# Reordering the head of a fused retention and gated MLP kernel: w_in's u half cast by GpSimd alone, the split of b behind the second k cast, centring as a step of its own

## The chip, the cores and the metric

The kernel runs on one core of one Trainium2 chip. The metric is the device time of one execution in microseconds (us), as the median of several runs. The core's engines are TensorE (PE in the profile; its weight loads are PEld), VectorE (DVE), ScalarE (ACT) and GpSimd (POOL); SyncE (SP) issues most transfers. Each engine works through its own queue in order and waits on semaphores for the others.

## The reference, cut to what matters

Retention (attention with a decay per head in place of a softmax) over q, k, v of shape 8 x 8 x 576 x 64, then a gated MLP whose gate mixes positions:

```
ret = (q k^T / 8) * gamma_h^(t-s)  for t >= s, else 0
x   = (ret v), heads side by side                 # 8 x 576 x 512
h   = gelu_tanh(x @ w_in)                         # w_in 512 x 1024
u, v = h[..., :512], h[..., 512:]
v_n = (v - mean(v)) / sqrt(var(v) + 1e-6) * g_ln
v_s = w_sg @ v_n (over positions, 576 x 576) + b_sg
out = x + (u * v_s) @ w_out                       # w_out 512 x 512
```

Inputs and output are float32; the matrix products inside are bf16.

## The kernel before, in words

**Tiling.** The positions of a batch are a lead of 64 and two blocks of 256. The leads of four batches are put together as one block, so the eight batches give 18 blocks j: block 0 is the leads of batches 0 to 3, blocks 1 and 2 are batch 0, 3 and 4 are batch 1, and so on. A block has two chunks c of 128 positions each.

**Stages of a block.** `load` issues the transfers of k, q and v. `cast(j, part, engine)` scales q and k by powers of gamma and turns them into bf16 (L263, a product with a table), v by a plain copy (L245). `T` transposes q or k on TensorE (`tp`) and copies it to SBUF (ScalarE for k, VectorE for q). `Sc(j, g)` makes scores for half of the heads and VectorE multiplies them by the causal mask (L300, `ret`). `Z(j, c)` adds to the running state and copies it to `zb`. `inter` and `intra` form the outputs from the state and from the masked scores; the end of `intra` copies them to `xT`, chunk 0 by ScalarE and, in the first three blocks, chunk 1 by VectorE.

**Stages of a chunk.** `V(j, c)` multiplies by the v half of w_in (L365) and applies the activation (L368, `vg`). `stats` takes mean and variance on VectorE (L376 to L380, `rs`) and then centres and scales by g (L385, `vc`); `power` raises the variance to -1/2 on GpSimd (L372, called pow below); `norm` multiplies the two on ScalarE (L393, L397, `vnm` and `vn`). `U(j, c)` is the u half (L414, L417). `W(b, c, half)` multiplies the normalized v of a batch by the transposed w_sg (`wT`, and `wL` for the lead, which also carries b; L434) and VectorE multiplies by u (L436, `gT`). `O` is the output product (L443) and the residual (L446), copied by ScalarE and stored.

**Weights.** w_in is loaded in two halves as float32 (`wst`), v half first, and cast to bf16 in four pieces. `split_b` clears the unused halves of `wL` and splits b into three bf16 parts `bp` (L169 to L176). `place_b(e)` issues three small transfers from `bp` into `wL[e]` on the GpSimd queue (L191). `load_w(j)` issues the transfers of w_sg there (L198), and `build_wT` transposes it on TensorE (L205), copied out by VectorE or ScalarE through a pool of two PSUM buffers that `T` and `Sc` use as well.

**Order.** The schedule is manual: engines take instructions in the order of the calls. Blocks 0 to 2, the head, are written out call by call (from L480 on). From block 3 on a loop interleaves the stages, with W and O products drawn from a list. `spin(n)` is n matmuls on zeros whose result isn't used. Steps registered with `later(n, f)` run after n calls of `tick`, which T, V, U, W and O make at their ends; in the head `stats_of`, `pow_of` and `norm_of` hold the steps of chunk 2j + c instead, and are called by hand. Chunk 1 (of block 0) is left to ticks 14, 16 and 18 after the head.

**Names in the argument.** "Cast 2k" is `cast(2, "k", ...)`; "pow2", "vc2" and "rs2" are the steps of chunk 2 (block 1, c = 0), and likewise chunks 3, 4 and 5. The first W in TensorE's order multiplies with wT[0] to wT[3] and then wL[0]; its "fourth matmul" needs the last transposed weight and the `vn` of chunk 5.

Of the kernel before, what the change touches and what calls it, by code (L numbers as in the profile page):

```python
# [13 lines left out]
I32 = mybir.dt.int32  # L14
# [5 lines left out]
def kernel(  # L20
# [12 lines left out]
    nc = tc.nc  # L33
# [6 lines left out]
    GB, LEAD, NT, MID = 4, 64, 9, 4  # L40
# [7 lines left out]
    consts = ctx.enter_context(tc.tile_pool(name="consts", bufs=1))  # L48
# [46 lines left out]
    srow_i = consts.tile([128, 3, 2], I32, name="srow_i")  # L95
    nc.gpsimd.iota(srow_i[:, 0], pattern=[[1, 2]], base=0, channel_multiplier=2)
    nc.gpsimd.iota(srow_i[:, 1:], pattern=[[256, 2], [1, 2]], base=LEAD, channel_multiplier=2)

    srow_i = consts.tile([128, 3, 2], I32, name="srow_i")
    nc.gpsimd.iota(srow_i[:, 0], pattern=[[1, 2]], base=0, channel_multiplier=2)  # L100
    nc.gpsimd.iota(srow_i[:, 1:], pattern=[[256, 2], [1, 2]], base=LEAD, channel_multiplier=2)
# [34 lines left out]
    w_stage = {}  # L136
# [31 lines left out]
    def split_b():  # L168
        nc.gpsimd.memset(wL[0][64:], 0.0)  # L169
        nc.gpsimd.memset(wL[1][:64], 0.0)  # L170
        rest = bs
        for n in range(3):
            nc.gpsimd.tensor_copy(bp[:, n, :], rest[:])
# [10 lines left out]
    def fill_first():  # L184
        nc.gpsimd.memset(vnm[0][0][64:], 1.0)
        nc.gpsimd.memset(vnm[0][1][:64], 1.0)

    def place_b(e):
        for n in range(3):
            r = 64 * (1 - e) + n  # L190
            nc.gpsimd.dma_start(wL[e][r:r + 1, :], bp[:SB * 2 - 1, n, :] if e else bp[1:, n, :])  # L191
# [39 lines left out]
    def later(n, fn):  # L231
        pend.append([n, fn])
        pend.sort(key=lambda e: e[0])
# [13 lines left out]
    def cast(j, part, eng):  # L247
        s = blk.setdefault(j, {})
        qk, vf = loaded[j]
        b, half = place(j)[1:]  # L250
        kind = 0 if b is None else 1 + half
        if part == "q":
            dst, src, tab = w2.tile([128, 2, H, D], BF, name="qb"), qk[:, 0], gq
        else:
            pool = consts if b is None else w3
            dst = pool.tile([128, 2, H, D], BF, name=part + ("lead" if b is None else "b"))
            src, tab = (qk[:, 1], gk) if part == "k" else (vf[:], None)
        s[part + "b"] = dst
        o = dst[:].rearrange("p a h d -> p h a d")
        if tab is None:  # L260
            copy(eng, o, src)
        else:
            eng.tensor_tensor(o, src, tab[:, kind].rearrange("p a h -> p h a").unsqueeze(3).to_broadcast(  # L263
                [128, H, 2, D]), op=Alu.mult)
# [94 lines left out]
    stats_of, pow_of, norm_of = {}, {}, {}  # L359

    def V(j, c, wait=(2, 4)):
        p, m = chunk(j, c)
        hv = psD.tile([128, F2], F32, name="hv", tag="d")
        for kk in range(KK):
            nc.tensor.matmul(hv[:], xTs[p][:, kk, 128 * m:128 * m + 128], w_in[:, kk, F2:],  # L365
                             start=(kk == 0), stop=(kk == KK - 1))
        vg = vgp.tile([128, F2], F32, name="vg")
        nc.scalar.activation(vg[:], hv[:], Act.Gelu_apprx_tanh)  # L368
        st = {}

        def power():
            nc.gpsimd.tensor_tensor(st["rs"][:], st["rs"][:], mhalf[:], op=Alu.pow)  # L372

        def stats():
            bst = w3.tile([128, 6], F32, name="bst")
            nc.vector.bn_stats(bst[:], vg[:])  # L376
# [3 lines left out]
            nc.vector.tensor_scalar(rs[:], mv[:, 1:2], 1e-6, None, op0=Alu.add)  # L380
            st["rs"] = rs
            if wait:
                power()
            vc = w2.tile([128, F2], F32, name="vc")
            nc.vector.scalar_tensor_tensor(vc[:], vg[:], mv[:, 0:1], g_bc[:], op0=Alu.subtract, op1=Alu.mult)  # L385
            st.update(vc=vc)

        def norm():
            rs, vc = st["rs"], st["vc"]
            if m == MID:  # L390
                for e in range(2):
                    half = slice(64 * e, 64 * e + 64)
                    nc.scalar.mul(vnm[p % 3][e][half], vc[half], rs[half])  # L393
                vns[p, m] = vnm[p % 3]
            else:
                vn = vnp.tile([128, F2], BF, name="vn")
                nc.scalar.mul(vn[:], vc[:], rs[:])  # L397
                vns[p, m] = [vn, vn]

        if wait:  # L400
            later(wait[0], stats)
            later(wait[1], norm)
        else:
            stats_of[2 * j + c], pow_of[2 * j + c], norm_of[2 * j + c] = stats, power, norm
        tick()

    def U(j, c):
# [79 lines left out]
    T(0, "q")  # L487
    spin(3)
    cast(0, "v", nc.gpsimd)
    split_b()  # L490
    Sc(0, 0)
    Sc(0, 1)
    Z(0, 1)
# [4 lines left out]
    inter(0)  # L498
    intra(0)
    load(3)  # L500
    nc.gpsimd.memset(wnat[:, :, 0:64], 0.0)
    place_b(0)
    cast(1, "q", nc.vector)
    build_g()
    V(0, 0, None)
# [1 line left out]
    T(1, "k")  # L507
    T(1, "q")
    cast(1, "v", nc.gpsimd)
    spin(2)  # L510
    Sc(1, 0)
    Z(1, 0)
    cast(2, "k", nc.gpsimd)
# [9 lines left out]
    for j in range(SB):  # L523
        load_w(j)
    cast(2, "v", nc.gpsimd)
    for n in range(2):
        (nc.gpsimd.tensor_copy if n else nc.scalar.copy)(w_in[:, :, 256 * n:256 * n + 256], w_stage[0][:, :, 256 * n:256 * n + 256])
    V(1, 0, None)
    Sc(2, 0)
    V(1, 1, None)  # L530
    Z(2, 0)
    inter(2)
    fill_first()
    stats_of[0]()
    pow_of[0]()
    Sc(2, 1)
    Z(2, 1)
    cast(3, "k", nc.gpsimd)
    wb = ["L0", "L1"] + list(range(SB - 1))
    U(0, 0)  # L540
    norm_of[0]()
    stats_of[2]()
    pow_of[2]()
    U(0, 1)
    intra(2)
    U(1, 0)
    norm_of[2]()
    stats_of[3]()
    cast(3, "q", nc.gpsimd)
    pow_of[3]()  # L550
    V(2, 0, None)
    V(2, 1, None)
    load(5)
    build_wT(wb[0])
    norm_of[3]()
    U(1, 1)
    build_wT(wb[1])
    stats_of[4]()
    cast(3, "v", nc.gpsimd)
    place_b(1)  # L560
    pow_of[4]()
    build_wT(wb[2])
    U(2, 0)
    build_wT(wb[3])
    stats_of[5]()
    pow_of[5]()
    norm_of[4]()
    build_wT(wb[4])
    U(2, 1)
    build_wT(wb[5])  # L570
# [23 lines left out]
    cast(5, "v", nc.gpsimd)  # L594
    fill_consts()
    later(14, stats_of[1])
    later(16, pow_of[1])
    later(18, norm_of[1])

# [74 lines left out]
```

## Time and profile before

| | us |
|---|---|
| median of 3 runs | 234.67 |
| the three runs | 234.67, 234.17, 237.1 |
| profiled execution | 234.34 |
| its span, first to last instruction | 232.6 |
| TensorE busy in the span | 215.0 |
| VectorE / ScalarE / GpSimd busy | 165.8 / 134.7 / 129.4 |
| granted TensorE clock, mean | 0.995 of full |

A row of a timeline reads: start, duration (both us from the span's start), engine, line, operation, output and inputs by the program's names, shape, count, and in brackets how long the engine stood idle before it and what ended that wait. Rows with a count hold several instructions one after the other. A group of busy times by stage gives, for each stretch, its length and the busy time and instruction count of each engine, then the granted clock, the share of the DMA engines and GB/s.

### The profile page before, as it was taken

The numbers are of one execution on the slowest core, as the hardware profiler recorded it, in microseconds if no ns is written. First come the engines' busy times: TensorE is split into PE (matmuls) and PEld (weight loads), VectorE is DVE, ScalarE is ACT, GpSimd is POOL, SyncE is SP. The second block draws the span as 40 slices with busy tenths as digits, with TensorE's granted clock in tenths as the row PEclk, the third lists the DMA queues.
The fourth block names the chain that finished last, engine by engine and source line by source line (L and its number), as shares of the span: only waits on it lengthen the run. The fifth ranks groups of instructions, "written<-read, shape, count | busy, mean of one in ns | idle before, by whom it ended". The sixth has DMA issues, their size and how long they took to land.

```text
span 232.6 us, 8357 instructions
## 1 busy us (share of the span) xinstructions
PE 215.0 (92%) x3603; PEld 154.8 (67%) x3603; DVE 165.8 (71%) x357; ACT 134.7 (58%) x217; POOL 129.4 (56%) x130
## 2 busy tenths in 40 slices
PE   7796879789997999999999899999999999999991
PEld 3344476577776786777768677777777777667760
DVE  5476788688979896579767886779857985566320
ACT  5353568614669464946575757657394739466332
POOL 5298869799958485538555674939381611113000
PEclk9999999999999999999999999999999999999997
DMA  6999999999396993699249922869522003300344
GB/s 167 286 301 297 302 258 275 238 282 268 94 261 204 201 230 65 207 278 291 79 126 299 276 74 66 251 213 287 146 90 93 4 3 111 118 3 0 136 116 159
DMA packets 64261, 41.59 MB, mean 179 GB/s; under 512 B 2208, under 2 KB 58592, under 8 KB 64224
## 3 DMA queue, kind: packets, MB, share of 16 engines
q1 hardware_dynamic: 61664, 39.33, 62.6%
q0 software_dynamic: 1472, 1.20, 3.1%
q10 hardware_dynamic: 1088, 0.52, 1.0%
q8 instruction: 28, 0.46, 0.9%
q14 instruction: 9, 0.07, 0.1%
HBM read 32.79 MB, written 9.44 MB: 182 GB/s over the span
## 4 chain that ended last, share of the span: by engine, by line
PE 67%; ACT 7%; DVE 6%; DMA 6%; POOL 5%; SPq 5%; issue 1%; ACTq 1%; DVEq 0%; POOLq 0%
PE wp L434 15%; PE op L443 13%; PE hv L365 10%; PE hu L414 10%; PE tp L272 5%; SPq L91 5%; DMA wst<-in_moe_w_in_dram 4%; PE op L446 3%; POOL rs L372 3%; PE zp L321 3%; PE sc L296 3%; PE ot L348 3%; PE ot L337 3%; DMA qk<-in_q_dram 2%; DVE bst L376 2%; ACT vnm L393 2%
## 5 line engine op out<-in xcount | busy, mean ns | idle before, releaser
L372 POOL TENSOR_TENSOR rs<-rs,mhalf 128x1 f32<-128x1 f32 x36 | 33.0, 916 | 73.0 <-DVE rs L380 67.9
L300 DVE TENSOR_TENSOR ret<-sc,mask 128x512 bf16<-128x512 f32 x72 | 46.2, 684 | 12.9 <-PE sc L296 12.8
L434 PE MATMUL wp<-wT,vn 128*128 128x288 bf16 x256 | 41.7, 287 | 2.9 <-ACT vn L397 2.8
L436 DVE TENSOR_TENSOR gT<-wp,uT 128x288 bf16<-128x288 f32 x64 | 28.1, 453 | 16.8 <-PE wp L434 14.0
L365 PE MATMUL hv<-w_in,xT 128*128 128x512 bf16 x144 | 36.5, 379 | 2.4 <-ACT xT L245 2.4
L414 PE MATMUL hu<-xT,w_in 128*128 128x128 bf16 x576 | 37.8, 219 | 0.0
L443 PE MATMUL op<-w_out,gT 128*128 128x512 bf16 x144 | 37.1, 380 | 0.0
L414 PEld LDWEIGHTS <-w_in 128*128 128x128 bf16 x576 | 34.0, 98 | 1.9
L368 ACT ACTIVATE vg<-hv 128x512 f32<-128x512 f32 x36 | 21.4, 596 | 22.5 <-PE hv L365 22.3
L376 DVE BATCH_NORM_STATS2 bst<-vg 128x6 f32<-128x512 f32 x36 | 24.8, 689 | 12.1 <-ACT vg L368 11.9
L449 ACT COPY ob<-op 128x512 f32<-128x512 f32 x36 | 20.9, 586 | 20.5 <-PE op L446 18.0
L263 POOL TENSOR_TENSOR kb<-qk,gk 128x1024 bf16<-128x1024 f32 x16 | 31.1, 1941 | 2.8 <-DMA qk<-in_k_dram 2.8
L397 ACT ACTIVATE vn<-vc,rs 128x512 bf16<-128x512 f32 x32 | 23.1, 722 | 14.4 <-POOL rs L372 12.4
L434 PEld LDWEIGHTS <-vn 128*128 128x128 bf16 x256 | 23.8, 98 | 10.7 <-ACT vn L397 3.7
L385 DVE SCALAR_TENSOR_TENSOR vc<-vg,mv,g_bc 128x512 f32<-128x512 f32 x36 | 29.9, 830 | 0.2 <-issue 0.2
L263 POOL TENSOR_TENSOR qb<-qk,gq 128x1024 bf16<-128x1024 f32 x15 | 28.9, 1929 | 0.0
L417 ACT ACTIVATE uT<-hu 128x512 bf16<-128x512 f32 x36 | 21.7, 602 | 11.5 <-PE hu L414 11.5
L245 ACT CAST xT<-ot 128x512 bf16<-128x512 f32 x33 | 22.0, 733 | 1.8 <-PE ot L348 1.6
L245 ACT COPY kT<-tp 128x1024 bf16<-128x1024 bf16 x18 | 18.1, 1008 | 8.3 <-PE tp L272 8.3
L365 PEld LDWEIGHTS <-xT 128*128 128x128 bf16 x144 | 12.8, 98 | 13.7 <-ACT xT L245 4.0
L443 PEld LDWEIGHTS <-gT 128*128 128x128 bf16 x144 | 12.3, 98 | 9.5
L434 PE MATMUL wp<-wL,vnm 128*128 128x288 bf16 x64 | 18.4, 287 | 0.0
(95 smaller groups left out, 290.0 us busy)
## 6 DMA issues: line engine op xcount, KB each, us to landing
qk<-in_k_dram SPq DMA_DIRECT2D x16, 512.0 KB, 8.2
qk<-in_q_dram SPq DMA_DIRECT2D x16, 512.0 KB, 7.5
vf<-in_v_dram SPq DMA_DIRECT2D x16, 512.0 KB, 7.6
out_dram<-ob SPq DMA_DIRECT2D x32, 256.0 KB, 2.5
wst<-in_moe_w_in_dram SPq DMA_DIRECT2D x2, 1024.0 KB, 7.3
vf<-in_v_dram SPq DMA_DIRECT2D x8, 128.0 KB, 4.3
out_dram<-ob SPq DMA_DIRECT2D x8, 128.0 KB, 2.4
qk<-in_k_dram SPq DMA_DIRECT2D x6, 128.0 KB, 3.4
```

The costliest lines, as they stand in the source:

```text
L245: (eng.copy if eng is nc.scalar else eng.tensor_copy)(o, i)
L263: eng.tensor_tensor(o, src, tab[:, kind].rearrange("p a h -> p h a").unsqueeze(3).to_broadcast([128, H, 2, D]), op=Alu.mult)
L300: nc.vector.tensor_tensor(s["ret"][:, r, 2 * g:2 * g + 2], sc[r][:], msk[:].unsqueeze(1).to_broadcast([128, 2, 2, 128]), op=Alu.mult)
L365: nc.tensor.matmul(hv[:], xTs[p][:, kk, 128 * m:128 * m + 128], w_in[:, kk, F2:], start=(kk == 0), stop=(kk == KK - 1))
L372: nc.gpsimd.tensor_tensor(st["rs"][:], st["rs"][:], mhalf[:], op=Alu.pow)
L376: nc.vector.bn_stats(bst[:], vg[:])
L385: nc.vector.scalar_tensor_tensor(vc[:], vg[:], mv[:, 0:1], g_bc[:], op0=Alu.subtract, op1=Alu.mult)
L397: nc.scalar.mul(vn[:], vc[:], rs[:])
L414: nc.tensor.matmul(hu[:, c, :], w_in[:, kk, 128 * c:128 * c + 128], xTs[p][:, kk, 128 * m:128 * m + 128], start=(kk == 0), stop=(kk == KK ...
L434: nc.tensor.matmul(ps[:], vns[p, m][e][:, 128 * c:128 * c + 128], w, start=(x == 0), stop=(x == SB - 1))
L436: nc.vector.tensor_tensor(gTs[p][:, c, col:col + HS], ps[:], uTs[p][:, c, col:col + HS], op=Alu.mult)
L443: nc.tensor.matmul(op[:], gTs[p][:, c, r], w_out[:, c, :], start=(c == 0), stop=False, skip_group_check=True)
```

## The change

- A repeated pair of iotas that fill `srow_i` is removed.
- `split_b` no longer clears `wL`; that and the clearing of w_sg's padding (`wnat`) are a function `clear_wL`, called where `split_b` was, behind cast 0v. `split_b` is called behind cast 1k on GpSimd, after `load(3)`.
- `place_b(0)` moves from there to behind cast 1v; the spin(2) at that place is removed.
- Both pieces of w_in's u half are cast by GpSimd; ScalarE did the first. `fill_first` (two clearings of `vnm`) moves ahead of them.
- Centring is taken out of `stats` as a step `centre`. For chunk 2 it is called behind `intra(2)`, for the others in the head right behind the statistics, with pow behind it; for chunk 1 it has a tick of its own.
- Casts 3k, 3q and 3v move behind the pow steps of chunks 2, 3 and 4; the statistics of chunks 4 and 5 move ahead of the second and the fourth `build_wT`. `place_b(1)` now follows pow5.

```
--- before.py
+++ after.py
@@ -91,10 +91,6 @@
                 nc.sync.dma_start(dst[:], src[b, :, s0:s0 + 256, :].rearrange("h (p a) d -> p h (a d)", a=2))
 
     load(0, (k, q))
-
-    srow_i = consts.tile([128, 3, 2], I32, name="srow_i")
-    nc.gpsimd.iota(srow_i[:, 0], pattern=[[1, 2]], base=0, channel_multiplier=2)
-    nc.gpsimd.iota(srow_i[:, 1:], pattern=[[256, 2], [1, 2]], base=LEAD, channel_multiplier=2)
 
     srow_i = consts.tile([128, 3, 2], I32, name="srow_i")
     nc.gpsimd.iota(srow_i[:, 0], pattern=[[1, 2]], base=0, channel_multiplier=2)
@@ -165,9 +161,12 @@
     wL = [consts.tile([128, S], BF, name=f"wL{e}") for e in range(2)]
     bp = consts.tile([SB * 2, 3, 64], BF, name="bp")
 
-    def split_b():
+    def clear_wL():
         nc.gpsimd.memset(wL[0][64:], 0.0)
         nc.gpsimd.memset(wL[1][:64], 0.0)
+        nc.gpsimd.memset(wnat[:, :, 0:64], 0.0)
+
+    def split_b():
         rest = bs
         for n in range(3):
             nc.gpsimd.tensor_copy(bp[:, n, :], rest[:])
@@ -356,7 +355,7 @@
             x = xTs[p][:, :, 128 * m:128 * m + 128].rearrange("p k (t a) -> p k a t", a=2)
             copy(nc.vector if j < 3 and c == 1 else nc.scalar, x, ot[c][:])
 
-    stats_of, pow_of, norm_of = {}, {}, {}
+    stats_of, pow_of, cen_of, norm_of = {}, {}, {}, {}
 
     def V(j, c, wait=(2, 4)):
         p, m = chunk(j, c)
@@ -378,9 +377,13 @@
             nc.vector.bn_aggr(mv[:], bst[:])
             rs = w3.tile([128, 1], F32, name="rs")
             nc.vector.tensor_scalar(rs[:], mv[:, 1:2], 1e-6, None, op0=Alu.add)
-            st["rs"] = rs
+            st.update(rs=rs, mv=mv)
             if wait:
                 power()
+                centre()
+
+        def centre():
+            mv = st["mv"]
             vc = w2.tile([128, F2], F32, name="vc")
             nc.vector.scalar_tensor_tensor(vc[:], vg[:], mv[:, 0:1], g_bc[:], op0=Alu.subtract, op1=Alu.mult)
             st.update(vc=vc)
@@ -401,7 +404,9 @@
             later(wait[0], stats)
             later(wait[1], norm)
         else:
-            stats_of[2 * j + c], pow_of[2 * j + c], norm_of[2 * j + c] = stats, power, norm
+            parts = stats, power, centre, norm
+            for d, f in zip((stats_of, pow_of, cen_of, norm_of), parts):
+                d[2 * j + c] = f
         tick()
 
     def U(j, c):
@@ -487,7 +492,7 @@
     T(0, "q")
     spin(3)
     cast(0, "v", nc.gpsimd)
-    split_b()
+    clear_wL()
     Sc(0, 0)
     Sc(0, 1)
     Z(0, 1)
@@ -498,8 +503,7 @@
     inter(0)
     intra(0)
     load(3)
-    nc.gpsimd.memset(wnat[:, :, 0:64], 0.0)
-    place_b(0)
+    split_b()
     cast(1, "q", nc.vector)
     build_g()
     V(0, 0, None)
@@ -507,7 +511,7 @@
     T(1, "k")
     T(1, "q")
     cast(1, "v", nc.gpsimd)
-    spin(2)
+    place_b(0)
     Sc(1, 0)
     Z(1, 0)
     cast(2, "k", nc.gpsimd)
@@ -523,48 +527,53 @@
     for j in range(SB):
         load_w(j)
     cast(2, "v", nc.gpsimd)
+    fill_first()
     for n in range(2):
-        (nc.gpsimd.tensor_copy if n else nc.scalar.copy)(w_in[:, :, 256 * n:256 * n + 256], w_stage[0][:, :, 256 * n:256 * n + 256])
+        nc.gpsimd.tensor_copy(w_in[:, :, 256 * n:256 * n + 256], w_stage[0][:, :, 256 * n:256 * n + 256])
     V(1, 0, None)
     Sc(2, 0)
     V(1, 1, None)
     Z(2, 0)
     inter(2)
-    fill_first()
     stats_of[0]()
-    pow_of[0]()
+    cen_of[0]()
     Sc(2, 1)
     Z(2, 1)
-    cast(3, "k", nc.gpsimd)
+    pow_of[0]()
     wb = ["L0", "L1"] + list(range(SB - 1))
     U(0, 0)
     norm_of[0]()
     stats_of[2]()
-    pow_of[2]()
     U(0, 1)
     intra(2)
+    cen_of[2]()
+    pow_of[2]()
+    cast(3, "k", nc.gpsimd)
     U(1, 0)
     norm_of[2]()
     stats_of[3]()
-    cast(3, "q", nc.gpsimd)
+    cen_of[3]()
     pow_of[3]()
     V(2, 0, None)
     V(2, 1, None)
+    cast(3, "q", nc.gpsimd)
     load(5)
     build_wT(wb[0])
     norm_of[3]()
+    stats_of[4]()
+    cen_of[4]()
     U(1, 1)
     build_wT(wb[1])
-    stats_of[4]()
+    pow_of[4]()
+    stats_of[5]()
+    cen_of[5]()
     cast(3, "v", nc.gpsimd)
+    pow_of[5]()
     place_b(1)
-    pow_of[4]()
     build_wT(wb[2])
     U(2, 0)
+    norm_of[4]()
     build_wT(wb[3])
-    stats_of[5]()
-    pow_of[5]()
-    norm_of[4]()
     build_wT(wb[4])
     U(2, 1)
     build_wT(wb[5])
@@ -594,6 +603,7 @@
     cast(5, "v", nc.gpsimd)
     fill_consts()
     later(14, stats_of[1])
+    later(15, cen_of[1])
     later(16, pow_of[1])
     later(18, norm_of[1])
 
```

More of the change, by code (lines that the diff above doesn't have):

```diff
@@ L403, in V @@
         else:
-            stats_of[2 * j + c], pow_of[2 * j + c], norm_of[2 * j + c] = stats, power, norm
+            parts = stats, power, centre, norm
+            for d, f in zip((stats_of, pow_of, cen_of, norm_of), parts):
+                d[2 * j + c] = f
         tick()
@@ L500 @@
     load(3)
-    nc.gpsimd.memset(wnat[:, :, 0:64], 0.0)
-    place_b(0)
+    split_b()
     cast(1, "q", nc.vector)
@@ L509 @@
     cast(1, "v", nc.gpsimd)
-    spin(2)
+    place_b(0)
     Sc(1, 0)
@@ L525 @@
     cast(2, "v", nc.gpsimd)
+    fill_first()
     for n in range(2):
-        (nc.gpsimd.tensor_copy if n else nc.scalar.copy)(w_in[:, :, 256 * n:256 * n + 256], w_stage[0][:, :, 256 * n:256 * n + 256])
+        nc.gpsimd.tensor_copy(w_in[:, :, 256 * n:256 * n + 256], w_stage[0][:, :, 256 * n:256 * n + 256])
     V(1, 0, None)
@@ L532 @@
     inter(2)
-    fill_first()
     stats_of[0]()
-    pow_of[0]()
+    cen_of[0]()
     Sc(2, 1)
     Z(2, 1)
-    cast(3, "k", nc.gpsimd)
+    pow_of[0]()
     wb = ["L0", "L1"] + list(range(SB - 1))
@@ L542 @@
     stats_of[2]()
-    pow_of[2]()
     U(0, 1)
     intra(2)
+    cen_of[2]()
+    pow_of[2]()
+    cast(3, "k", nc.gpsimd)
     U(1, 0)
@@ L548 @@
     stats_of[3]()
-    cast(3, "q", nc.gpsimd)
+    cen_of[3]()
     pow_of[3]()
@@ L552 @@
     V(2, 1, None)
+    cast(3, "q", nc.gpsimd)
     load(5)
@@ L596 @@
     later(14, stats_of[1])
+    later(15, cen_of[1])
     later(16, pow_of[1])
```

28 lines of the change are left out of this document (16 added, 12 removed).

## The prediction

> **What bounds the kernel now.** I read the engine totals first, then busy time by stage, then the timelines of each engine up to 61 us, where every edit lies.
>
> ```profile
> span 232.6 us, 8357 instructions
> PE 215.0 (92%) x3603; PEld 154.8 (67%) x3603; DVE 165.8 (71%) x357; ACT 134.7 (58%) x217; POOL 129.4 (56%) x130
> ...
> 27.00:37.00 10.00, 7.67 (x158) 5.54 (x157) 9.02 (x17) 7.50 (x13) 7.41 (x7) 1.00 1.08 250
> ...
> 45.00:56.00 11.00, 10.20 (x221) 8.13 (x220) 9.19 (x19) 3.36 (x4) 10.82 (x10) 1.00 1.11 260
> ```
>
> A stage row gives its bounds, its length, busy us of PE, PEld, DVE, ACT and POOL, the granted clock, the DMA share and GB/s. TensorE sets the end, so a change in the head counts by what it does to TensorE's start into its dense part. But from 45 to 56 us GpSimd is busy 10.82 of 11 us: its queue of casts can be as binding as TensorE there. Four places of the head decide:
>
> ```profile
> 18.97 1.04 POOL L245 CAST vb<-vf 128x1024 bf16<-128x1024 f32 x1 [0.18 <-DMA vf<-in_v_dram]
> 20.80 1.93 POOL L263 TENSOR_TENSOR kb<-qk,gk 128x1024 bf16<-128x1024 f32 x1 [0.79 <-DMA qk<-in_k_dram]
> ...
> 22.78 0.62 PE L272 MATMUL tp<-ident,kb 128*128 128x128 bf16 x8 [0.77 <-POOL kb L263]
> 26.76 1.04 PE L365 MATMUL hv<-w_in,xT 128*128 128x512 bf16 x4
> ...
> 27.40 1.04 ACT L527 CAST w_in<-wst 128x1024 bf16<-128x1024 f32 x1 [2.02 <-DMA wst<-in_moe_w_in_dram]
> 28.36 1.08 ACT L368 ACTIVATE vg<-hv 128x512 f32<-128x512 f32 x2
> 29.32 0.37 ACT L245 CAST zb<-zp 128x256 bf16<-128x256 f32 x1
> ...
> 29.75 0.47 PE L337 MATMUL ot<-qT,zb 64*64 64x128 bf16 x10 [1.53 <-ACT zb L245]
> ...
> 44.69 0.30 PE L434 MATMUL wp<-wT,vn 128*128 128x288 bf16 x1 [1.51 <-ACT vn L397]
> ```
>
> Cast 1v waits for its load until 18.97. TensorE waits for cast 2k at 22.78. At 29.75 it waits 1.53 us for `zb`, which stood on ScalarE behind a w_in copy that waited 2.02 us for its load. At 44.69 the first gating product waits 1.51 us for the last `vn`.
>
> **A resource that the edits shift.** VectorE's centring (`vc`, L385) takes 0.74 us alone and longer whenever a GpSimd cast is running as it starts:
>
> ```profile
> 29.08 0.74 DVE L385 SCALAR_TENSOR_TENSOR vc<-vg,mv,g_bc 128x512 f32<-128x512 f32 x1
> ...
> 32.29 1.93 POOL L263 TENSOR_TENSOR kb<-qk,gk 128x1024 bf16<-128x1024 f32 x1 [2.04 <-DMA qk<-in_k_dram]
> 32.80 1.96 DVE L385 SCALAR_TENSOR_TENSOR vc<-vg,mv,g_bc 128x512 f32<-128x512 f32 x1
> ...
> 56.51 1.93 POOL L263 TENSOR_TENSOR qb<-qk,gq 128x1024 bf16<-128x1024 f32 x1
> 57.87 1.11 DVE L385 SCALAR_TENSOR_TENSOR vc<-vg,mv,g_bc 128x512 f32<-128x512 f32 x1
> 60.44 0.44 DVE L436 TENSOR_TENSOR gT<-wp,uT 128x288 bf16<-128x288 f32 x1
> 60.98 1.03 PE L443 MATMUL op<-w_out,gT 128*128 128x512 bf16 x4
> ```
>
> The cast at 32.29 ends at 34.22 and the held centring at 34.76; the one at 56.51 ends at 58.44, its centring at 58.98. Both end 0.54 after the cast: the centring does not run beside it, it waits for its end. Behind the second one stand the masks, a copy and the last gating product's multiply (60.44 to 60.88), and TensorE's first output product starts at 60.98, just behind it. So that product's start hangs on the end of cast 6q.
>
> **The change, part by part.**
>
> *Nothing at either end.* The two iotas removed ran before GpSimd's long wait for the first values, so the load hides them; without that cover they would cost a fraction of a microsecond:
>
> ```profile
> 0.83 0.13 POOL L96 IOTA srow_i<- 128x2 int32 x1 [0.40 <-POOLq L658]
> 10.26 1.04 POOL L245 CAST vlead<-vf 128x1024 bf16<-128x1024 f32 x1 [6.14 <-DMA vf<-in_v_dram]
> ```
>
> For chunk 1, whose steps are due by ticks, centring moves one tick later; counting calls, no other VectorE instruction comes between the two ticks, so the order there is as before: nothing. The spin(2) removed fills time in which TensorE waits anyway (its copy of block 1 follows); gaps of 1.53 us stand in a stage with granted clock 1.00, and the longest I expect is 1.6: nothing.
>
> *b behind cast 1k.* The five small instructions and the clearing:
>
> ```profile
> 12.50 0.23 POOL L173 CAST bp<-bs 10x64 bf16<-10x64 f32 x1
> ...
> 14.01 1.03 POOL L494 CAST w_in<-wst 128x1024 bf16<-128x1024 f32 x1
> 15.01 1.92 POOL L263 TENSOR_TENSOR kb<-qk,gk 128x1024 bf16<-128x1024 f32 x1
> 16.88 0.35 POOL L501 MEMSET wnat<- 128x320 bf16 x1
> 17.18 1.60 POOL L191 DMA_DIRECT2D wL<-bp  x3
> ```
>
> Splitting took from 12.50 to 14.01, 1.5 us. Ahead of cast 1k the 0.35 clearing takes its place. That cast ends between 15.7 (if its load is there) and 16.93 (as now), with the split behind it between 17.2 and 18.4: before 18.97 either way, so the load of v1 hides it. TensorE's block 1 may start half a microsecond earlier, but its state product needs vb, which the load fixes: nothing gained. But the three issues of `place_b(0)` (1.60) move behind cast 1v, and cast 2k is queued behind them: 18.97 + 1.0 + 1.65 = 21.6 instead of 20.80. **Cost 0.8 us** at TensorE's 22.78, which becomes 23.6, and for V(1,0) and V(1,1) after it.
>
> *u half on GpSimd alone.* ScalarE no longer waits for w_in. V(1,1) (26.76) now ends at 27.8; with the 0.8 it ends at 28.6, its activation starts at 28.65, `zb` half a microsecond on at 29.15 (0.54 apiece for the two activations at 28.36), instead of 29.32. TensorE's 29.75 becomes 29.6: of the 1.0 us copy taken off, 0.8 has paid for place_b: **gain 0.15**.
>
> ```profile
> 22.67 2.75 POOL L198 DMA_DIRECT2D wnat<-in_moe_w_sg_dram  x5
> ...
> 27.43 1.04 POOL L527 CAST w_in<-wst 128x1024 bf16<-128x1024 f32 x1 [0.96 <-DMA wst<-in_moe_w_in_dram]
> 28.53 0.52 POOL L185 MEMSET vnm<- 64x512 bf16 x1
> 29.60 0.65 POOL L372 TENSOR_TENSOR rs<-rs,mhalf 128x1 f32<-128x1 f32 x1
> 30.85 1.96 PE L414 MATMUL hu<-xT,w_in 128*128 128x128 bf16 x32
> ```
>
> GpSimd: cast 2k 21.6, five issues to 26.2, cast 2v (1.0 to 1.1) to 27.3, the two vnm clearings (1.07 from 28.53 to 29.60; they fill the old wait) to 28.4, then 28.4 to 30.4 for both w_in casts, where the second used to be ready at 28.47. U(0,0) would ask at 30.85 - 0.15 = 30.7: hidden, by 0.3.
>
> *Centring.* `vc` of chunk 0 was computed at 29.08; now it is ready 0.8 later, at 29.9, inside the second w_in cast, and ends 0.55 after it: 31.0. The masks of Sc(2,1) follow (1.2), then the statistics of chunk 2 (1.0 to `rs`, as from 41.66 to 42.66 below): rs2 at 33.1 to 33.2. The 1.2 is the pair of masks at 30.59 (1.29, the next starting a little before its recorded end).
>
> ```profile
> 30.59 1.29 DVE L300 TENSOR_TENSOR ret<-sc,mask 128x512 bf16<-128x512 f32 x2 [0.78 <-PE sc L296]
> ...
> 34.69 0.72 DVE L245 CAST xT<-ot 128x512 bf16<-128x512 f32 x1
> ...
> 41.66 0.68 DVE L376 BATCH_NORM_STATS2 bst<-vg 128x6 f32<-128x512 f32 x1
> 42.66 0.15 DVE L380 TENSOR_SCALAR rs<-mv 128x1 f32<-128x1 f32 x1
> 43.40 0.55 DVE L245 COPY wT<-wtp 128x576 bf16<-128x576 bf16 x2
> ...
> 38.97 1.63 POOL L191 DMA_DIRECT2D wL<-bp  x3
> 42.97 0.92 POOL L372 TENSOR_TENSOR rs<-rs,mhalf 128x1 f32<-128x1 f32 x1 [1.39 <-ACT wT L245]
> 43.85 1.93 POOL L263 TENSOR_TENSOR kb<-qk,gk 128x1024 bf16<-128x1024 f32 x1
> ```
>
> The copy of attention outputs, held to 34.69 by the centring that took 1.96, goes ahead of it at 33.2; the centring follows at 33.85. GpSimd does pow2 at 33.4 and cast 3k only then (34.1 to 34.5, by whether it waits for this centring; it was at 32.29). Then the two queues alternate: vc3 waits for cast 3k (to about 36.8), vc4 for cast 3q (to 39.7), `rs` of chunk 5 comes at r = 41.1 where it was 42.66. From r, with steps as above: pow5 at r + 0.3, place_b(1) 0.92 on, cast 4k 1.65 on: r + 2.9 = **44.0, where it was 43.85**. TensorE: centring and the first transposed-weight copy (0.8 + 0.55), five transposes and the next copy (1.1): the fourth gating matmul at r + 2.55 = **43.65, where it was 44.69**, 1.05 earlier.
>
> *Where that gain goes.* From 44.69 to the centring at 57.87 nothing on TensorE and VectorE waits for GpSimd, so that centring is ready 13.18 after the fourth matmul: 56.8. GpSimd works without a gap from 43.85 to cast 6q at 56.51, 12.66: now 56.7. The cast is first by 0.15, the centring waits for its end as now, and TensorE's output product, ready a microsecond earlier, waits for the multiply behind it. The microsecond is idle time in front of 60.98, and what is left is the shift of GpSimd's queue: 0.15 by the sum, 0.3 if cast 3k waits for vc2. I take **+0.2 us**; from there on all goes as before. The profiled execution took 234.34 (1.74 outside its span), 0.33 under the median 234.67: 234.54, and 234.9 on the median's scale.
>
> *The rule beside these rows.* The Trainium skill, page "SBUF — State Buffer", section "Who interferes with whom", says that a VectorE instruction with two SBUF inputs and a GpSimd one that reads SBUF exclude each other, the first to issue holding the port to its end. The trace agrees (both held centrings ended 0.54 after the cast). By that rule it is order of issue that decides at 34 us and at 56.7, as in the two rivals that follow.
>
> **Rivals.**
>
> *Centring first at 56.7.* If the fourth matmul comes 0.15 earlier against GpSimd than summed, the centring starts before cast 6q, ends after 0.74 us, and masks and multiply run a microsecond early: the output product keeps nearly all of the 1.05. For it: the margin is smaller than the errors of a sum of a dozen steps. Against: the margin is r + 15.75 against r + 15.6, whatever r is. 234.67 - 1.0 = 233.7.
>
> *Slower: cast 3k ahead of vc2.* pow2 took 0.65 when nothing disturbed it (29.60), so cast 3k can start at 34.0, 0.15 behind vc2. If the attention outputs come 0.2 later, or GpSimd is served first at pow2's end, vc2 waits for the whole cast and ends at 36.5 instead of 34.6, with the statistics of chunk 3 behind it, and pow3 on GpSimd behind those: both queues 1.7 late to r. Cast 4k at 45.7, cast 6q at 58.4, the output product at 62.8. That is 1.85 over before, 236.5. It decides from the point where `ot` of block 2 is finished after 33.4. Against: TensorE would have to lose the 0.15 and more.
>
> *w_in late.* If the two casts on GpSimd are held themselves, U(0,0) waits for them past 30.7; up to 0.5 us later this moves the masks and rs2 by no more than that: 234.9 + 0.5 = 235.4 at most. It stays within the forecast's own range.
>
> **How the numbers follow.** Forecast 234.9 (own range 234.2 to 235.4): 0.45. Centring first, 233.2 to 234.1: 0.28. Cast 3k first, 235.8 to 237: 0.17. Something not named: 0.10, half on either side. The range takes in the first two and half of the third, 233.2 to 236.4. Two per cent, about what a measurement of this kernel can tell from no change, is 4.7 us: no case reaches it, and I leave 0.03 for faster and 0.05 for slower.
>
> **What would show it.** In the changed profile: cast 2k at 21.6 and its transposes at 23.6; `zb` near 29.2; both w_in casts from 28.4 to 30.4 and a centring over 1 us at 29.9; the copy of attention outputs at 33.2 ahead of its centring; cast 4k at 44.0; the fourth gating matmul near 43.7, and a new idle of about 1 us on TensorE before the first output product, which starts at 61.1. I am wrong if that product starts at 60 (centring first) or after 62 (cast 3k first), or if time changes behind 61 us, where no order is touched.

## The result, and the profile after

The changed kernel is **slower by 0.6%**: median 236.32 us (20 runs) against 234.90 us (20 runs), ratio 1.0057, interval 1.0036 to 1.0079. The interval is clear of 1, and the difference is far under 2%. The profiled execution took 237.24 us. The forecast had 234.9 (0.2 us over before) with 233.2 to 236.4 for the range: the time lies at its upper edge, and most of the 1.35 us of the ratio comes from places that the forecast costed at nothing or gave to a rival.

From the page of the changed kernel, totals and the granted clock in 40 slices of 5.9 us, and busy times by stage (columns as before):

```profile
span 235.5 us, 8351 instructions
...
PE 217.8 (92%) x3601; PEld 156.9 (67%) x3601; DVE 167.4 (71%) x357; ACT 134.0 (57%) x216; POOL 131.0 (56%) x129
...
PEclk9997699999999999999999999999999999999999
```

```profile
20.00:22.00 2.00, 0.92 (x8) 0.78 (x9) 0.93 (x2) 0.00 (x0) 1.56 (x3) 0.61 0.89 255
22.00:25.00 3.00, 2.59 (x78) 2.40 (x78) 1.34 (x3) 0.37 (x1) 2.99 (x4) 0.50 0.85 245
25.00:28.00 3.00, 2.64 (x49) 1.78 (x47) 3.00 (x3) 1.38 (x2) 3.00 (x7) 0.62 0.97 306
```

Two things are new. From 20 to 28 us TensorE's granted clock is 0.50 to 0.62; in the profile of before it was 1.00 there. And the first trace met late loads: cast 1v, which waits for its load, starts at 20.77 where it was 18.97. What the order of the edits does is therefore read from a second trace of the same kernel, whose loads came as early as before (19.01). Its timeline, in the order of the prediction's steps:

```profile
19.01 1.04 POOL L244 CAST vb<-vf 128x1024 bf16<-128x1024 f32 x1 [0.58 <-DMA vf<-in_v_dram]
21.61 1.95 POOL L262 TENSOR_TENSOR kb<-qk,gk 128x1024 bf16<-128x1024 f32 x1
23.61 1.03 PE L271 MATMUL tp<-ident,kb 128*128 128x128 bf16 x8 [1.56 <-POOL kb L262]
28.39 2.01 POOL L532 CAST w_in<-wst 128x1024 bf16<-128x1024 f32 x2
31.60 0.47 PE L336 MATMUL ot<-qT,zb 64*64 64x128 bf16 x10 [0.53 <-ACT zb L244]
34.96 0.55 POOL L371 TENSOR_TENSOR rs<-rs,mhalf 128x1 f32<-128x1 f32 x1 [1.86 <-DVE rs L379]
35.32 0.74 DVE L244 CAST xT<-ot 128x512 bf16<-128x512 f32 x1 [0.44 <-PE ot L347]
35.48 1.93 POOL L262 TENSOR_TENSOR kb<-qk,gk 128x1024 bf16<-128x1024 f32 x1
35.95 2.01 DVE L388 SCALAR_TENSOR_TENSOR vc<-vg,mv,g_bc 128x512 f32<-128x512 f32 x1
46.84 1.95 POOL L262 TENSOR_TENSOR kb<-qk,gk 128x1024 bf16<-128x1024 f32 x1
59.23 2.72 DVE L388 SCALAR_TENSOR_TENSOR vc<-vg,mv,g_bc 128x512 f32<-128x512 f32 x1
59.47 1.92 POOL L262 TENSOR_TENSOR qb<-qk,gq 128x1024 bf16<-128x1024 f32 x1
62.60 0.61 PE L271 MATMUL tp<-ident,kb 128*128 128x128 bf16 x8 [1.56 <-DVE ret L299]
63.93 1.03 PE L448 MATMUL op<-w_out,gT 128*128 128x512 bf16 x4
```

Up to TensorE's transposes at 23.61 every step is within 0.01 us of the sum (cast 2k 21.6, transposes 23.6; the pair of w_in casts 28.39 to 30.40). Then the state product that waits for `zb` comes at 31.60 where 29.6 was forecast: TensorE's matmuls between run at half speed (the transposes at 23.61 take 1.03 us, before 0.62). The attention outputs come at 35.32 instead of 33.2; cast 3k has got in ahead of the centring of chunk 2, which takes 2.01 us; cast 4k is at 46.84 instead of 44.0; and the centring at 59.23 is held by cast 6q for 2.72 us, with TensorE idle for 1.56 us behind it. The first output product starts at 63.93 instead of 61.1.

A distance is more robust than a start, since the loads of the head come up to 2 us later in one execution than in another. From cast 1v to the first output product it was 42.0 before and is 44.9 here.

### The profile page after: what moved, and what is told of

Read it like the earlier page. It is cut to its first block, busy times and chain, and to the rows that moved or that the text cites. A ratio compares the mean times of both kernels' runs of the same rounds, so it can differ in the third digit from the quotient of the medians.

```text
span 235.5 us, 8351 instructions
## 1 busy us (share of the span) xinstructions
PE 217.8 (92%) x3601; PEld 156.9 (67%) x3601; DVE 167.4 (71%) x357; ACT 134.0 (57%) x216; POOL 131.0 (56%) x129
## 4 chain that ended last, share of the span: by engine, by line
PE 69%; DVE 9%; DMA 7%; ACT 7%; POOL 4%; issue 2%; ACTq 1%; DVEq 0%; POOLq 0%
PE wp L439 14%; PE op L448 13%; PE hv L364 11%; PE hu L419 9%; DMA qk<-in_q_dram 7%; PE tp L271 6%; PE sc L295 3%; PE op L451 3%; POOL rs L371 3%; PE ot L347 3%; PE zp L320 3%; PE ot L336 3%; DVE bst L375 2%; DVE vc L388 2%; ACT vnm L396 2%
## 5 line engine op out<-in xcount | busy, mean ns | idle before, releaser
L388 DVE SCALAR_TENSOR_TENSOR vc<-vg,mv,g_bc 128x512 f32<-128x512 f32 x36 | 31.6, 879 | 0.2 <-issue 0.2
L295 PE MATMUL sc<-qT,kT 64*64 64x128 bf16 x576 | 17.5, 223 | 1.3 <-DVE qT L244 1.0
```

Source lines behind the costliest of these rows:

```text
L295: nc.tensor.matmul(sc[r][cc, x, a, :], kT[rr, a, kk, cc], qT[rr, :, kk, cc], start=True, stop=True, skip_group_check=True)
```

## The experiments

All but run 5 were timed in rounds beside the kernel before; ratios are to that kernel. Runs 1 to 4, 6 to 8 and 9 to 12 were timed together, with medians of 234.82, 235.23 and 235.35 for the kernel before, so between these groups the ratios are to be compared. Clock and distance are those of one trace each. "Product" is the start of the first output product.

| kernel | median us | ratio | interval | clock 20 to 24 / 24 to 28 us | cast 1v to product, us |
|---|---|---|---|---|---|
| before, second trace | (one run) 233.89 | | | 1.00 / 1.00 | 41.4 |
| changed, again | 236.24 | 1.0060 | 1.0033 to 1.0088 | 0.76 / 0.50 | 44.9 |
| changed + spin(2) | 236.13 | 1.0049 | 1.0019 to 1.0079 | 0.93 / 0.64 | 44.3 |
| changed, vc2 first | 235.25 | 1.0024 | 0.9997 to 1.0052 | 0.89 / 0.50 | 44.1 |
| changed, fills behind 6q | 235.65 | 1.0035 | 1.0006 to 1.0064 | 0.68 / 0.50 | 42.8 |
| changed, TensorE kept busy | 234.95 | 1.0007 | 0.9982 to 1.0032 | 1.00 / 1.00 | 43.2 |
| changed, place_b(0) later | 235.10 | 1.0014 | 0.9980 to 1.0048 | 0.82 / 0.75 | 43.5 |
| before + split edit | 235.76 | 1.0036 | 1.0003 to 1.0069 | 0.91 / 0.67 | 43.1 |
| before + order edit | 235.09 | 0.9996 | 0.9962 to 1.0030 | 1.00 / 1.00 | 42.0 |
| before + w_in edit | 234.20 | 0.9943 | 0.9910 to 0.9976 | 1.00 / 1.00 | 43.4 |
| changed, busy + vc2 first | 234.38 | 0.9975 | 0.9941 to 1.0009 | 1.00 / 1.00 | 42.0 |
| changed, all cures | 234.22 | 0.9944 | 0.9911 to 0.9978 | 1.00 / 1.00 | 39.8 |

**1. The changed kernel again.** No edit.

> The changed kernel again, for a second trace of it: in the first one the loads of the head came 1.8 us later than in the profile of before (cast 1v at 20.77 where it was 18.97) and TensorE's granted clock fell to 0.5 to 0.62 from 20 to 28 us. If the loss is made by the order of the edits (my theory: vc2 held by cast 3k, then the centring of block 3 held by cast 6q), it stands here without late loads too: 1.3 us over before, vc2 longer than 1.5 us, the centring before the first output product longer than 2 us. If the loss is that of the loads and the clock (rival), a trace with early loads has vc2 and that product where the prediction put them (61.1) and the time is that of before.

The loss stands without late loads: ratio 1.0060, vc2 2.01 us, the later centring 2.72 us. The clock fell here too, so this run does not part order from clock. It shows where it fell. Busy time of TensorE (the first number behind the length) in two stretches of 3.4 us, first in the second trace of the changed kernel, then in the first of before:

```profile
18.60:22.00 3.40, 1.88 (x80) 1.54 (x80) 1.45 (x3) 0.37 (x1) 2.98 (x5) 1.00 1.17 284
20.10:23.50 3.40, 1.52 (x64) 1.27 (x63) 1.89 (x4) 0.74 (x2) 3.39 (x5) 0.79 0.99 272
```

```profile
18.60:22.00 3.40, 2.45 (x84) 1.67 (x81) 2.17 (x4) 0.60 (x2) 2.43 (x3) 1.00 1.21 288
20.10:23.50 3.40, 2.20 (x74) 1.83 (x74) 2.80 (x5) 0.74 (x2) 2.71 (x3) 1.00 1.15 307
```

The first stretch, 1.88 of 3.4 us busy where it was 2.45, is the one without spin(2); the clock is still 1.00 in it and falls at its end, with the wait for cast 2k (22.0 to 23.6) only beginning.

The place of the fall follows a grid. In each of the fourteen traces every change of the granted clock lies a whole number of steps of 3.41 us from its first one. The steps of run 1 around the fall:

```profile
18.66:22.07 3.41, 1.87 (x80) 1.48 (x79) 1.52 (x3) 0.37 (x1) 3.05 (x5) 1.00 1.16 283
22.07:25.48 3.41, 1.65 (x10) 1.13 (x11) 2.58 (x3) 1.11 (x2) 3.41 (x5) 0.50 0.94 305
```

Where the steps lie against the start of the program differs from trace to trace, so the same work can fill one step thinly in one execution and be shared by two in another.

**2. spin(2) put back.**

```
     place_b(0)
+    spin(2)
     Sc(1, 0)
```

> The changed kernel with spin(2) put back behind place_b(0). Rival (the clock that falls when TensorE idles is the loss): granted clock 1.00 from 20 to 28 us, and some 1.3 us faster than the changed kernel, that is the time of before. My theory: no part of the loss, within 0.3 us of the changed kernel; TensorE waits there for loads and casts whatever its clock.

As my theory said, it brings next to nothing (1.0049). But not for the reason given: in this trace the clock fell all the same, at 23.5 us, at the end of a step that has most of the wait for cast 2k (22.3 to 23.9) in it. That this is 1.4 us later than in run 1 is not shown to be the work of spin(2): in run 8, without it, the steps lay much the same and the clock fell at 23.3.

Its stages:

```profile
20.10:23.50 3.40, 1.52 (x64) 1.27 (x63) 2.09 (x5) 0.74 (x2) 3.39 (x5) 1.00 1.02 270
24.00:28.00 4.00, 3.51 (x51) 2.35 (x52) 1.73 (x3) 1.74 (x2) 3.94 (x7) 0.64 1.09 338
```

So the run shows that spin(2) alone does not reliably keep the clock up, and nothing on what a fallen clock costs. Run 6 does that.

**3. vc2 ahead of the copy of attention outputs.**

```
     stats_of[2]()
+    cen_of[2]()
     U(0, 1)
     intra(2)
-    cen_of[2]()
```

> The changed kernel with the centring of chunk 2 called right behind its statistics again, ahead of the copy of attention outputs. My theory (cast 3k holds it in the changed order): vc2 takes 0.74 us again instead of 2.01, statistics of chunk 3 come 1.3 to 1.6 us earlier, cast 4k too, and the kernel is 1.0 to 1.5 us faster than the changed one, about before. Rival (place_b and the clock are the loss): within 0.3 us of the changed kernel.

The timeline of this kernel, VectorE's centring of chunk 2 and GpSimd's pow and cast behind it:

```profile
35.73 0.74 DVE L388 SCALAR_TENSOR_TENSOR vc<-vg,mv,g_bc 128x512 f32<-128x512 f32 x1
35.90 0.99 POOL L371 TENSOR_TENSOR rs<-rs,mhalf 128x1 f32<-128x1 f32 x1 [1.86 <-DVE rs L379]
36.85 1.93 POOL L262 TENSOR_TENSOR kb<-qk,gk 128x1024 bf16<-128x1024 f32 x1
```

0.74 us instead of 2.01, and 1.0 us faster than the changed kernel in the same group (ratios 1.0024 and 1.0060, with overlapping intervals). The held centring's time is shown by the trace; that it is a part of the loss, near the size expected, is what the medians say, and the intervals leave its size open.

**4. The clearings of fill_consts behind cast 6q.**

```
-    fill_consts()            # ahead of the loop
...
             cast(j + 3, "q", nc.gpsimd)
+            if j == HEAD:
+                fill_consts()
```

> The changed kernel with the four clearings of fill_consts moved behind cast 6q, so that this cast ends 2.2 us earlier and the centring of block 3 before the first output product finds GpSimd at work that only writes. My theory: that centring takes 0.74 us instead of 2.72, TensorE's wait of 1.56 us in front of it goes, and the kernel is about 1.5 us faster than the changed one, 0.1 under before. Rival (the loss is made before 45 us alone): within 0.4 us of the changed kernel, since GpSimd has as much to do as before and the wait turns up behind it.

Its timeline, the two centrings of block 3, the product, and TensorE's next wait:

```profile
59.03 0.74 DVE L388 SCALAR_TENSOR_TENSOR vc<-vg,mv,g_bc 128x512 f32<-128x512 f32 x1
62.03 1.03 PE L448 MATMUL op<-w_out,gT 128*128 128x512 bf16 x4
62.66 2.50 DVE L388 SCALAR_TENSOR_TENSOR vc<-vg,mv,g_bc 128x512 f32<-128x512 f32 x1
67.00 1.04 PE L364 MATMUL hv<-w_in,xT 128*128 128x512 bf16 x4 [0.58 <-ACT xT L244]
```

The centring at 59.03 takes 0.74 us and the product comes 2.1 us sooner after cast 1v than in run 1. But the median falls by 0.6 us only: the next centring (62.66) is now the one held, 2.50 us by cast 6k, and TensorE waits 0.58 us at 67.00. The wait was moved, and most of the gain at the product is not found in the time; the rival's "within 0.4" was too little, my 1.5 too much.

**5. The kernel before, a second trace.** No edit.

> The kernel before once more, for a second trace of it. Theory: TensorE's granted clock stays at 1.00 from 16 to 32 us and the first output product starts near 61.0, as in the first trace (the four traces with the changed order all show 0.5 to 0.76 somewhere from 24 to 28 us, the one of before none). Rival: the first trace of before was lucky, and this one shows a fallen clock in the head as well and that product at 62 or later.

Clock 1.00 throughout, product at 60.55. So neither trace of before loses its clock in the head. But both, at 234.34 and 233.89, are faster than the median of its runs, so traces compared alone overstate the loss.

The mean granted clock of every timed execution is on record too, and it says that the two traces are lucky ones. The traces without a fall ahead of the program's end have a mean of 0.995 to 1.000, those with one 0.983 to 0.993. Of the 99 executions of before in the three groups, 26 have 0.994 or more, 70 have 0.991 or less, and 30 of these 0.987 or less; of the 32 of the changed kernel, none, 23 and 22. So the kernel before loses its clock in many executions too, mostly for a shorter time; where, its two traces don't show. In the first group the median of the 10 executions of before at 0.985 or less is 235.86, that of the 14 at 0.994 or more 233.70. By this a part of the clock's price is in the time of before already.

One more thing differs between the two traces of before: chunk 2's centring took 1.96 us behind cast 3k in the first and 0.74 at 32.37 here, since cast 3k came only at 32.83.

**6. TensorE kept busy while it waits.**

```
     place_b(0)
+    spin(2)
     Sc(1, 0)
...
     cast(2, "q", nc.vector)
+    spin(5)
     T(2, "k")
```

> The changed kernel with spin(2) put back in front of Sc(1,0) and spin(5) added in front of the transposes of k of block 2, where TensorE waits 1.56 us for cast 2k. Nothing on GpSimd changes, so cast 2k is as late as before (21.6 plus what the load of v1 is late). Theory (the wait lets the clock fall, and the next 6 us of TensorE work run at half speed): granted clock 1.00 from 24 to 28 us, the state product of block 2 (the one that waits for zb) near 30.0 instead of 31.6 on a load of v1 at 19.0, and 1.0 to 1.8 us faster than the changed kernel. Rival (the lateness of cast 2k alone, and the held centrings): within 0.4 us of the changed kernel.

Stages of this kernel, and rows of its timeline from cast 2k to the centring of chunk 2:

```profile
20.10:23.50 3.40, 2.40 (x68) 1.68 (x68) 2.40 (x5) 0.74 (x2) 3.39 (x5) 1.00 1.16 317
24.00:28.00 4.00, 3.47 (x70) 2.15 (x71) 2.37 (x3) 1.97 (x3) 3.94 (x7) 1.00 1.13 333
```

```profile
22.03 1.95 POOL L262 TENSOR_TENSOR kb<-qk,gk 128x1024 bf16<-128x1024 f32 x1
24.04 0.62 PE L271 MATMUL tp<-ident,kb 128*128 128x128 bf16 x8 [0.38 <-POOL kb L262]
30.00 0.47 PE L336 MATMUL ot<-qT,zb 64*64 64x128 bf16 x10 [0.53 <-ACT zb L244]
33.66 0.55 POOL L371 TENSOR_TENSOR rs<-rs,mhalf 128x1 f32<-128x1 f32 x1 [1.86 <-DVE rs L379]
33.71 0.74 DVE L244 CAST xT<-ot 128x512 bf16<-128x512 f32 x1
34.18 1.93 POOL L262 TENSOR_TENSOR kb<-qk,gk 128x1024 bf16<-128x1024 f32 x1
34.34 2.32 DVE L388 SCALAR_TENSOR_TENSOR vc<-vg,mv,g_bc 128x512 f32<-128x512 f32 x1
```

Cast 2k is as late as before (2.6 us after cast 1v in both), but the clock stays at 1.00, the state product comes at 30.00, 10.6 us after cast 1v instead of 12.6, and the kernel is 1.3 us faster than the changed one (1.0007 against 1.0060, intervals apart) and level with before. **The fallen clock is a loss by itself, and the largest single one measured**, though the interval of run 3 takes in a like gain. All 12 executions of this kernel have a mean clock of 0.991 or more. That is better than before's, so being level in time does not mean that nothing but the clock was lost. The held centring is still there, at a full clock: the outputs come at 33.71, and cast 3k starts 0.16 us before the centring.

**7. place_b(0) behind pow of chunk 0.**

```
     cast(1, "v", nc.gpsimd)
-    place_b(0)
...
     pow_of[0]()
+    place_b(0)
```

> The changed kernel with place_b(0) moved behind pow of chunk 0, where GpSimd is idle for some 1.9 us, so that cast 2k follows cast 1v at once. Theory: TensorE's wait for cast 2k falls from 1.56 to 0.8 us, its transposes start 0.8 us earlier against the load of v1, the clock holds, and the kernel is 1.5 to 2.0 us faster than the changed one, 0.2 to 0.6 under before. Rival (the loss is the held centrings only): 0.8 us earlier in the head at most, and within 0.4 us of the changed kernel at the end.

The wait fell to 0.69 us as expected, but the clock held only in part (0.82 and 0.75): the spins are missing in this kernel too. It is 1.1 us faster than the changed one by the ratios and not below before: the direction of the theory, with somewhat over half of its size.

**8. The split edit alone on the kernel before** (clear_wL, split_b behind cast 1k, place_b(0) behind cast 1v, spin(2) removed).

> The kernel before with one part of the change alone: clearing split off, the split of b behind cast 1k, place_b(0) behind cast 1v, spin(2) removed. Theory: this part makes most of the loss: cast 2k 0.8 us late, clock down to 0.5 or so from 24 to 28 us, 1.0 to 1.8 us slower than before. Rival (the loss comes from the order of centring and casts): 0.2 us slower at most, since the w_in copy on ScalarE waits for its load until 27.4 anyway and hides the 0.8.

Clock 0.91 and 0.67, cast 2k 2.6 us after cast 1v, 0.36% slower (0.03 to 0.69). It lies clear of 1, but 0.36% is 0.8 us, under the 1.0 to 1.8 expected, and the interval, from 0.1 to 1.6 us, takes in the rival's 0.2 too. This part makes a loss by itself, and its trace shows the same fall of the clock.

**9. The order edit alone on the kernel before** (centring as a step, casts behind the pow steps, statistics moved; the repeated iotas are gone here as well).

> The kernel before with the last part of the change alone: centring as a step of its own, casts 3k, 3q, 3v behind the pow steps, statistics of chunks 4 and 5 earlier; b, place_b(0), spin(2) and w_in as before. Theory: the clock stays at 1.00 from 16 to 32 us, since cast 2k is on time; vc2 is held by cast 3k all the same and takes about 2.0 us, and the centring of block 3 is held by cast 6q for more than 2 us, so that the first output product starts 0.8 to 1.6 us later than the 60.55 to 60.98 of the two traces of before; 0.5 to 1.2 us slower than before. Rival (all of the loss is the clock): within 0.3 us of before.

Its timeline, cast 3k with vc2 and the centring of block 3 with cast 6q:

```profile
33.34 1.92 POOL L261 TENSOR_TENSOR kb<-qk,gk 128x1024 bf16<-128x1024 f32 x1
33.94 1.88 DVE L387 SCALAR_TENSOR_TENSOR vc<-vg,mv,g_bc 128x512 f32<-128x512 f32 x1
57.09 2.72 DVE L387 SCALAR_TENSOR_TENSOR vc<-vg,mv,g_bc 128x512 f32<-128x512 f32 x1
57.33 1.93 POOL L261 TENSOR_TENSOR qb<-qk,gq 128x1024 bf16<-128x1024 f32 x1
```

Both held centrings are there at a clock of 1.00: vc2 with 1.88 us, the later one with 2.72. Yet the time is that of before: by the time, the rival is right. Product less cast 1v is 42.0 as in the first trace of before. That fits what the forecast said of the order: a gain of TensorE up to 45 us, spent at cast 6q. (Here the fourth gating matmul starts 0.79 us ahead of cast 4k, at 43.91 and 44.70; in the first trace of before it was 0.84 behind it.)

**10. The w_in edit alone on the kernel before.**

```
-        (nc.gpsimd.tensor_copy if n else nc.scalar.copy)(w_in[...], w_stage[0][...])
+        nc.gpsimd.tensor_copy(w_in[...], w_stage[0][...])     # fill_first() ahead of it
```

> The kernel before with the w_in part of the change alone: both pieces of the u half cast by GpSimd, the clearing of vnm ahead of them. Theory: ScalarE no longer waits for w_in, the state product of block 2 starts 0.6 to 0.9 us earlier than the 29.32 to 29.75 of before, but the first output product hangs on cast 6q and with it on GpSimd's queue, which has 1.0 us more to do: that product within 0.5 us of before and the time within 0.4 us of before. Rival (TensorE's start into its dense part sets the end): 0.6 to 0.9 us faster.

0.57% faster (0.24 to 0.90), where I had expected no more than 0.4 us: the rival's number, but not its reason. The trace (235.36, over the median; its clock is 0.84 and 0.79 up to 20 us, since it fell for 6.8 us at 10.8, behind a wait of TensorE of 1.97 us for VectorE's first cast of q, 7.43 to 9.40) shows no gain at the product. It shows one at the end. After ScalarE's last copy (the last row of its timeline) the program goes on to the end of the span for 3.5 us, where it was 4.3 before. The row of that copy, and from the page the queue that brings instructions (packets, MB, share):

```profile
228.82 1.29 ACT L449 COPY ob<-op 128x512 f32<-128x512 f32 x2 [0.88 <-DMA out_dram<-ob]
```

```profile
q14 instruction: 8, 0.07, 0.1%
```

The copies end at 230.11, the span at 233.6. The same two rows of the order edit alone (run 9), where ScalarE has one instruction more:

```profile
227.80 1.29 ACT L453 COPY ob<-op 128x512 f32<-128x512 f32 x2 [0.89 <-DMA out_dram<-ob]
```

```profile
q14 instruction: 9, 0.07, 0.1%
```

229.09 to 233.2 is 4.1. All four traces with the w_in copy on ScalarE (before twice, runs 8 and 9) have 4.1 to 4.3 us there and 9 instruction packets on that queue; all the others have 3.4 to 3.5 and 8. That the packet is the cause is argued only; no run removed an instruction of ScalarE elsewhere. And 0.8 us is 0.34%: what the rest of the 0.57% comes from is open.

**11. Both cures: TensorE kept busy, vc2 first.**

> The changed kernel with both cures: spins in front of Sc(1,0) and of the transposes of k of block 2, and the centring of chunk 2 right behind its statistics. Theory (two separate losses, 1.3 us for the clock and 1.0 us for vc2, as measured each alone): 2.0 to 2.5 us faster than the changed kernel, some 1 us under before (ratio near 0.996). Rival (both act on one chain, the end of cast 6q, and the second brings little): within 0.4 us of before.

The two nearly add up: 0.9975 against the 1.0060 of run 1, some 2.0 us (1.3 and 1.0 alone), with an interval that still takes in 1.

**12. All cures**: also place_b(0) behind pow of chunk 0, and the clearings behind cast 6v.

> As the kernel with both cures, and place_b(0) behind pow of chunk 0 (so that cast 2k follows cast 1v at once), and the four clearings of fill_consts behind cast 6v, so that casts 6q and 6k come 2.2 us earlier and end before the centrings of block 3 are ready. Theory: no centring of block 3 takes longer than 1.2 us, the first output product starts at 60.0 or earlier on a load of v1 at 19.0, and the kernel is 0.8 to 1.6 us faster than before (ratio 0.993 to 0.997). Rival: what is gained at that product is given back at the next centrings, as half of it was when the clearings stood behind cast 6q alone: within 0.4 us of the kernel with both cures.

Its timeline from the centring of block 3 on:

```profile
56.24 0.74 DVE L388 SCALAR_TENSOR_TENSOR vc<-vg,mv,g_bc 128x512 f32<-128x512 f32 x1
59.23 1.03 PE L448 MATMUL op<-w_out,gT 128*128 128x512 bf16 x4
62.53 0.55 POOL L371 TENSOR_TENSOR rs<-rs,mhalf 128x1 f32<-128x1 f32 x1
63.12 0.72 ACT L400 ACTIVATE vn<-vc,rs 128x512 bf16<-128x512 f32 x1 [1.88 <-POOL rs L371]
64.51 1.04 PE L364 MATMUL hv<-w_in,xT 128*128 128x512 bf16 x4 [1.35 <-ACT xT L244]
```

Faster than both kernels: 0.9944 (0.9911 to 0.9978), level with run 10. The product comes 39.8 us after cast 1v and no centring of block 3 is held for long. But 1.35 us goes back at 64.51: the clearings now stand ahead of pow (62.53), `vn` waits 1.88 us for it on ScalarE, and the attention outputs that TensorE needs stand behind that `vn`. Placing the clearings behind this pow was not tried.

## Why the prediction came out as it did

- **Right: cast 2k and the w_in casts.** 21.6, 23.6 and 28.4 to 30.4 were met to 0.01 us in the trace whose load of v1 came as before (19.01). Where the clock holds, the sum stands further on: in run 6, with that load 0.46 us later, the state product comes at 30.00 and chunk 0's centring takes 1.05 us at 30.32 (29.6 and "over 1 us at 29.9").
- **Wrong: "gaps ... the longest I expect is 1.6: nothing".** The step took the length of one gap as the measure, and counted spin(2) as mere filling of a wait. The stretches in run 1 show 1.88 and 1.52 of 3.4 us busy where it had been 2.45 and 2.20, and the clock fell. Run 6 puts the price at 1.3 us, as large as nearly all of the net loss. The Trainium skill, page "TensorE: Matmul & The Clock Gate", section "HAM oscillation — how this bites in real kernels", gives the rule as no idle gap over some 3.4 us. No gap between matmuls in the head was longer than 2.0 us in any trace (1.97 in run 10, 1.83 in the first trace of the changed kernel, 1.57 and less elsewhere) and the clock fell, so the measurement decides: it is the busy share of a stretch of that length that has to be watched.
- **Wrong: vc2 ahead of cast 3k.** The slower rival came true, in every trace of the changed order, at a full clock too. The place was right, the sign given for it (outputs later than 33.4) was not the whole of it. In run 1 the outputs are late, by the clock. In run 6, with everything 0.46 us later by the load, the copy of the outputs comes at 33.71, as the sum has it (33.66), and cast 3k is first all the same. Mis-sized are two terms of 0.1 to 0.25 us: pow2 takes 0.55 (34.96 to 35.48) where 0.65 was taken, and the outputs come 0.05 behind its start in run 6 (33.71, with pow2 at 33.66), not 0.2 ahead of it. The margin of 0.15 us was smaller than these errors. Price: 1.0 us by run 3, and run 6's product, less the 0.46, lies 1.1 behind the forecast's 61.1; the rival had put it at 1.6 over the forecast.
- **Right: the product hangs on cast 6q, and on nothing of TensorE.** From cast 4k to the product are 17.1 us in every trace in which the clearings stood where they were: 60.98 - 43.85, 63.93 - 46.84, and the same to 0.04 in ten others. TensorE's gain in the head was spent in front of it, as said, and when the clearings were moved the distance shrank (15.4 in runs 4 and 12).
- **Right in what came of it, wrong in what decides: who is first at cast 6q.** The forecast made it a matter of 0.15 us in the recorded starts. Its two distances were met (13.18 from the fourth gating matmul to the centring, 12.63 from cast 4k to cast 6q), but that matmul, at 46.05, is 0.79 us ahead of cast 4k where the sum had 0.35. So the condition of the rival "centring first" came true: in the second trace of the changed kernel the centring starts 0.24 us *ahead* of the cast (59.23 and 59.47). It still waits for the cast's end. So that rival could not win there, and a gain on TensorE made that wait longer, not shorter: 1.11 us before, 2.72 after.
- **Not foreseen: 0.8 us at the end of the program**, which came with the w_in edit and hides a part of the loss: the product is 3.4 us later than in the second trace of before and the span 2.6. By an estimate from these rows the time without it would have been 0.8 us longer, 237.1, beyond the range. That it lies inside is luck: the upper part of the range stood for half of the rival with cast 3k first, and the clock, measured as the larger loss, was put at nothing.

The three parts measured alone (+0.36%, -0.04%, -0.57%) do not add up to the +0.57% of the whole. Their sum is -0.25%, 0.8% short, which is more than the intervals of some 0.3% each explain together, so a part of this is open; what the traces show is that the parts meet on the same queues.

## What to carry to other kernels

When an edit lengthens a wait of the matrix engine in a loosely filled stage, price the clock as well as the wait, and look at the mean clock of the timed executions before a trace is taken for typical. Unneeded matmuls near the wait were not enough here (run 2); in the wait as well they were (run 6); in the wait alone was not tried. Where a cast queue on GpSimd runs without a gap, find the VectorE instruction with two SBUF inputs that meets it: here the end of that cast set the next stage, and work gained on TensorE only waited longer. After a reorder, compare distances from the last load that was waited for, not starts.

## What the runs showed of the hardware

- TensorE's granted clock changed only on a grid of 3.41 us. In eight traces it fell to half ahead of the program's end, for one or two steps, each time behind a step in which TensorE was busy 1.28 to 1.94 us, without any gap over 2.0 us; the least of the steps in the head behind which it stayed at 1.00 was 1.86 (run 12, at 7.3 us), then 2.08 (run 11, at 8.2 us). Later in the runs steps of 1.65 to 1.95 also kept it, though some matmuls can be missing from a trace. So by these traces no step of 2.0 us or more lost the clock, and between 1.65 and 1.94 both happened.
- A centring whose record begins 0.18 to 0.24 us before that of a cast already queued behind another GpSimd instruction lost to it (runs 1, 9 and 11: 2.72, 2.72, 2.66 us). The Trainium skill, page "SBUF — State Buffer", section "Who interferes with whom", lets the first to issue win; if so, the recorded start is not that moment, and no run shows which is. Clearings, which only write, did not hold a centring (0.74 us in run 4 with clearings running), as the page says.
- The span's end came 0.7 to 0.9 us sooner after the last copy in every kernel with one ScalarE instruction less (3.4 us in ten traces, 4.1 to 4.3 in four).
